# Values put in chunk order by transfers within SBUF instead of by TensorE, in a recurrent attention and token-mixing kernel

## The chip, the cores and the metric

The kernel runs on one core of a Trainium2 chip. The metric is the device time of one execution in microseconds, the median of the runs shown.

## The reference

For 4 batches, 8 heads, 768 tokens and a head size of 48, a recurrence with a decaying state is computed per head; its output, 384 wide per token, goes through a token-mixing layer.

```python
for t in range(S):
    cur = einsum('bhd,bhe->bhde', u[None] * kt, vt)
    y[:, :, t] = einsum('bhd,bhde->bhe', rt, state + cur)
    state = wt[:, :, :, None] * state + einsum('bhd,bhe->bhde', kt, vt)
x = y.transpose(0, 2, 1, 3).reshape(B, S, H * D)
W_tok = scale * einsum('bsd,btd->bst', x @ w_q, x @ w_k)
out = maximum(einsum('bst,btd->bsd', W_tok, x), 0.0) @ w_out
```

Inputs and output are float32. `u` is the bonus, one row of 48 per head.

## The kernel before

**Tiles.** A chunk is 128 tokens, a unit is 256 tokens of all 8 heads of one batch. There are 12 units, three to a batch, numbered n = 0 to 11. For a unit, w, k, r and v are loaded each as a tile of 128 partitions x 768 float32 (`load`, line 301): partition p holds tokens 2p and 2p+1 of every head side by side, so that a row in memory is 384 bytes. In this form a partition holds two tokens and the partitions 0 to 63 hold the first chunk, 64 to 127 the second. The computation wants one chunk of 128 tokens over the 128 partitions, even tokens on partitions 0 to 63 and odd ones on 64 to 127 ("chunk order").

**How w, k and r come there.** ACT takes the logarithm of w (`ln`); a product with a 0/1 matrix (`cw`) sums it along the tokens and puts it in order, and ACT takes both exponentials (`ep`, `en`). POOL casts k and r to bfloat16 (`k16`, `r16`), TensorE transposes them in quarters (`kT`, `rT`), a copy (`ks`) and DVE products (`qT`, `RT`, `KT`; most KT are on POOL) follow.

**How v comes there.** For units 0 to 8 POOL casts the value tile to `v16`, TensorE multiplies it with a permutation (`vp`, lines 585 to 597: four products with `PM`, form "E", or with quarters of the identity, form "e"), and ACT or DVE copies the result from PSUM to `VB` (line 598). For batch 3 (`WHOLE = (3,)`, units 9 to 11) all values of the batch come by `load_whole` (line 306): four transfers of 288 KB with 192-byte rows, one token per row, already in chunk order; POOL casts them to `VB` (line 575). `VB` feeds the state update (`sn`), the output product (`ya`) and, times `dd`, the bonus term `Vd` on POOL (line 618).

**The rest of a unit.** `dps` multiplies qT with the bonus `UB` (line 606), `dd` is its copy; `A` and `AM` are the masked scores, `kb` and `kd` the transposed keys, `sn` and `SB` the state passed to the next chunk, `yi` and `ya` the output in PSUM, `X` (DVE) its scaled sum with Vd, `xt` and `XT` its transpose, `qk` and `QK` the projections. After the third unit of a batch `T`, `TS`, `mx`, `rl`, `fp`, `os` do the mixing layer and `st` stores 384 KB of output for each unit.

**The bonus.** `uT` (line 281) is 128 x 8, filled by two transfers on the ACT queue with one element of 4 bytes a row (line 321); POOL casts it to `UB` (line 436).

**What sets the order.** Every operation is a step of a plan (class `Plan`, line 34). `RANK` gives each step its place in the queue of its engine: E TensorE, A ACT, D DVE, P POOL, S the issues of SP. `ALT` gives, letter by letter, the engine or form of the steps that have a choice; a lower-case e is a form of a TensorE step in quarters, and 30 warming products `z` are either run (E) or left out (e). Each engine works its queue strictly in order, and each waits for what its head step needs. A ring holds the buffers of a kind (`RINGS`, line 267): 4 for each of the loaded tiles, 2 for `v16`, `VB` and most others, 4 for `SB`. SP issues all loads and nearly all stores, in order; a load waits on SP until the ring has a free buffer. The numbers of nanoseconds in the steps serve only to write out the order of the program.

The head of the SP order before: wg0 kg0 rg0 vg0 kg1 wg1 rg1 vg1 wg2 kg2 rg2 vg2; its end: vg8 wg10 rg9 kg9 rg10 wg11 kg10, the four of the whole-batch values, st0, kg11 rg11, stores (w, k, r, v of a unit are wg, kg, rg, vg).

Of the kernel before, what the change touches and what calls it, by code (L numbers as in the profile page):

```python
# [33 lines left out]
class Plan:  # L34
# [51 lines left out]
    def order(self):  # L86
# [85 lines left out]
    3, 0, 0, 0, 5, 18, 0, 0, 21, 1, 2, 0, 0, 0, 1, 0, 0, 2, 0, 0, 3, 0, 0, 1, 3, 4, 4, 4, 2, 5,  # L172
    3, 5, 11, 3, 6, 4, 1, 5, 2, 5, 17, 8, 24, 9, 9, 10, 25, 10, 18, 7, 10, 6, 12, 7, 20, 8, 27,
    11, 30, 37, 33, 31, 15, 73, 31, 82, 32, 6, 0, 0, 4, 0, 0, 7, 0, 0, 8, 0, 0, 9, 6, 7, 26, 11,
    12, 23, 28, 10, 13, 12, 14, 8, 34, 14, 36, 15, 15, 40, 17, 45, 21, 41, 18, 48, 20, 53, 23,
    57, 64, 59, 58, 27, 74, 29, 87, 35, 9, 0, 0, 10, 0, 0, 11, 0, 0, 12, 0, 0, 13, 11, 12, 38,
    16, 17, 39, 42, 16, 18, 19, 14, 13, 47, 20, 49, 22, 18, 55, 24, 60, 25, 56, 22, 61, 26, 68,
    69, 72, 70, 30, 80, 36, 88, 36, 94, 38, 97, 40, 109, 49, 47, 0, 0, 102, 42, 120, 53, 50, 0,
    0, 134, 58, 141, 62, 51, 0, 0, 13, 0, 0, 14, 0, 0, 15, 0, 0, 17, 0, 0, 19, 16, 17, 50, 23,
    21, 63, 66, 25, 28, 29, 20, 19, 71, 28, 77, 33, 23, 75, 32, 79, 34, 76, 30, 81, 35, 85, 37,  # L180
    86, 91, 89, 90, 40, 100, 41, 104, 44, 16, 0, 0, 20, 0, 0, 22, 0, 0, 23, 0, 0, 24, 22, 25,
    67, 26, 27, 84, 93, 38, 42, 41, 39, 26, 95, 39, 110, 47, 32, 98, 47, 106, 49, 92, 37, 101,
    46, 105, 48, 115, 119, 118, 117, 54, 128, 59, 139, 60, 19, 0, 0, 21, 0, 0, 24, 0, 0, 25, 0,
    0, 31, 24, 27, 83, 34, 33, 96, 99, 43, 44, 45, 29, 28, 103, 43, 111, 48, 33, 113, 52, 108,
    50, 107, 45, 112, 51, 122, 124, 126, 125, 57, 138, 61, 156, 68, 164, 73, 167, 76, 185, 82,
    54, 0, 0, 176, 78, 211, 97, 52, 0, 0, 183, 81, 213, 99, 53, 0, 0, 26, 0, 0, 28, 0, 0, 27, 0,
    0, 31, 0, 0, 46, 31, 30, 116, 52, 51, 114, 121, 53, 56, 55, 34, 35, 129, 56, 136, 62, 40,
    131, 60, 140, 65, 127, 58, 135, 61, 143, 68, 149, 151, 153, 154, 73, 165, 75, 188, 86, 29,
    0, 0, 30, 0, 0, 33, 0, 0, 32, 0, 0, 50, 36, 38, 123, 55, 54, 132, 137, 57, 64, 63, 39, 37,
    142, 66, 159, 69, 47, 163, 76, 160, 75, 144, 67, 148, 70, 157, 74, 170, 172, 174, 175, 82,  # L190
    187, 83, 199, 91, 35, 0, 0, 37, 0, 0, 34, 0, 0, 38, 0, 0, 59, 41, 42, 145, 65, 64, 146, 150,
    69, 71, 72, 44, 43, 155, 67, 158, 70, 49, 177, 83, 166, 77, 161, 71, 168, 78, 179, 181, 184,
    182, 86, 191, 89, 205, 94, 212, 98, 223, 103, 237, 109, 55, 0, 0, 231, 105, 245, 111, 56, 0,
    0, 234, 109, 248, 113, 57, 0, 0, 36, 0, 0, 41, 0, 0, 40, 0, 0, 45, 0, 0, 46, 0, 0, 63, 46,
    45, 162, 72, 74, 169, 171, 79, 81, 80, 51, 53, 189, 84, 56, 195, 91, 186, 87, 190, 88, 194,
    90, 198, 92, 200, 203, 201, 204, 95, 210, 96, 221, 102, 39, 0, 0, 44, 0, 0, 42, 0, 0, 66,
    50, 48, 173, 77, 79, 178, 180, 80, 85, 84, 52, 54, 192, 87, 59, 207, 98, 197, 93, 193, 88,
    202, 94, 206, 96, 214, 217, 219, 216, 104, 226, 104, 233, 110, 43, 0, 0, 48, 0, 0, 49, 0, 0,
    85, 55, 57, 196, 92, 89, 93, 90, 208, 209, 95, 102, 99, 97, 100, 101, 58, 220, 101, 60, 61,
    215, 103, 224, 106, 218, 100, 222, 105, 225, 229, 227, 230, 228, 232, 107, 235, 106, 238,  # L200
    239, 112, 111, 108, 236, 107, 240, 241, 108, 113, 242, 244, 243, 110, 246, 114, 115, 250,
    253, 118, 116, 59, 0, 0, 61, 0, 0, 247, 112, 116, 251, 252, 114, 119, 58, 0, 0, 60, 0, 0,
    249, 117, 115, 254, 255, 117, 118, 119, 62, 0, 0, 6, 147, 19, 35, 13, 51, 65, 43, 44, 29,
    16, 2, 46, 78, 0, 21, 152, 52, 1, 62, 130, 32, 15, 8, 14, 54, 22, 9, 133, 7,
]
ALT = ("PPDEADAAEDAPPADEAAEAEAAPPDPEADAeDAAAAAAAAPPAPeADEAEAAPPDDEAAeAEDAPPDPeAAAEAAAAAAAAAPPDPE"
       "ADEDEAAPPAPeDAEDEAAPPDPeAAAEDAAAAAADAPPDPAeDEAAPPAPAEAeADPPAAAEADDEAADADDDAADADDAAAEeEEE"
       "eEEEEEeeEeeeEeeeeEeeEeeeE")
# [5 lines left out]
def kernel(  # L214
# [27 lines left out]
    WHOLE = (3,)  # L242
    DIRECT = (0, N - 1)

# [36 lines left out]
    uT = const([C, NP * 2], F32, "uT")  # L281
    UB = const([C, NP * 2], BF16, "UB")
# [31 lines left out]
    def setup():  # L314
# [4 lines left out]
        nc.vector.memset(uT, 0.0)  # L319
        for hh in range(2):  # L320
            nc.scalar.dma_start(out=view(uT, hh, [[2, NP], [1, 1]], p0=hh * 64, pn=D),
                                in_=dataclasses.replace(u, offset=hh * D,
                                                        ap=[[1, D], [D2, NP], [1, 1]]))
# [30 lines left out]
        nc.vector.memset(PM, 0.0)  # L354
# [62 lines left out]
    def weights():  # L417
        bq = Buf("none")

        def f(e):  # L420
            nc.sync.dma_start(out=view(wq_f, 0, [[DH, NK], [1, DH]]),
                              in_=moe_w_q.rearrange("(n p) h -> p n h", p=128))
            nc.sync.dma_start(out=view(wk_f, 0, [[DH, NK], [1, DH]]),
                              in_=moe_w_k.rearrange("(n p) h -> p n h", p=128))
            nc.sync.dma_start(out=view(wo_f, 0, [[DM, NK], [1, DM]]),
                              in_=moe_w_out.rearrange("(n p) d -> p n d", p=128))
        l = plan.dma(("wts",), 1800, 3300, f)[1]

        def cast(e):
            nc.gpsimd.tensor_scalar_mul(view(wq_sb, 0, [[128, NK], [64, 2], [1, DH]]),  # L430
                                        view(wq_f, 0, [[DH, NK], [0, 2], [1, DH]]), scale)
            nc.gpsimd.tensor_copy(wk_sb, wk_f)
            nc.gpsimd.tensor_copy(wo_sb, wo_f)
        wts["qk"] = wts["o"] = add(("wcast",), {"P": 2650}, cast, [l])
        wts["p"] = add(("pm",), {"P": 900}, lambda e: permute())
        wts["u"] = add(("ub",), {"P": 200}, lambda e: nc.gpsimd.tensor_copy(UB, uT))

    def unit(n, batch):
# [9 lines left out]
        for name, ap in (("wg", w), ("kg", k), ("rg", r)) + (() if whole else (("vg", v),)):  # L448
            g[name] = ring(name)
            g[name + "L"] = plan.dma((name, n), 570, 1190 + 250 * (n == 0 and name == 'kg') + 250 * (n > 2),  # L450
                                     lambda e, ap=ap, x=g[name].tile: load(b, i, x, ap),
                                     buf=g[name])[1]
# [61 lines left out]

        def transposed(name, src, step, place):
            def f(e):
                o = at(kr, BF16)
                for hp in range(NP):
                    for j in range(2):
                        for c in range(2):  # L520
                            mm(o[:, ds(c * 1024 + place + hp * C + j * 64, 64)],
                               src.tile[ds(c * 64, 64), ds(j * 512 + hp * 128, 128)],
                               ID16[ds(c * 64, 64), ds(c * 64, 64)], trans=True)
            return add((name, n), {"E": 245}, f, [step], kr, [src], mode=1)

        def turned(place, c0=0, nc_=2):
            return view(at(kr, BF16), c0 * 1024 + place, [[1024, nc_], [1, 512]])
        kTs = transposed("kT", k16, k16s, 0)
        rTs = transposed("rT", r16, r16s, 512)
# [7 lines left out]
                      view(qT.tile, 0, [[512, 2], [1, 512]]), turned(512),  # L537
# [5 lines left out]
        for cs in fine:  # L543
            n4 = NP * len(cs)

            def f_RT(e, cs=cs, n4=n4):
                o = view(RT.tile, cs[0] * 512, [[512, len(cs)], [64, H], [1, 64]])
                x = view(at(kr, BF16), cs[0] * 1024 + 512, [[1024, len(cs)], [64, H], [1, 64]])
                y = view(ep.tile, cs[0] * NP * EW, [[NP * EW, len(cs)], [66, H], [1, 64]])
                nc.vector.tensor_tensor(o, x, y, ALU.mult)  # L550
# [28 lines left out]
        else:  # L579
            v16, vp = ring("v16"), wide()  # L580
            v16s = add(("v16", n), {"P": 826}, lambda e: nc.gpsimd.tensor_copy(  # L581
                view(v16.tile, 0, [[D, H], [DM, 2], [1, D]]),
                view(g["vg"].tile, 0, [[D2, H], [D, 2], [1, D]])), [g["vgL"]], v16, [g["vg"]])

            def f_vp(e):
                x = at(vp)
                for j in range(2):
                    for c in range(2):
# [7 lines left out]
            vps = add(("vp", n), {"E": (330, 1, None), "e": (185, 3, None)}, f_vp,  # L596
                      [v16s, wts["p"]], vp, [v16])
            VBs = add(("VB", n), copies(2 * DM), lambda e: copy(
                e, view(VB.tile, 0, [[DM, 2], [1, DM]]), view(at(vp), 0, [[512, 2], [1, DM]])),
                [vps], VB, [vp])  # L600
# [3 lines left out]
        def f_dps(e):  # L604
            x = at(dps)
            for c in range(2):
                for hp in range(NP):
                    mm(x[:, ds(c * H + hp * 2, 2)], qT.tile[:, ds((c * NP + hp) * C, C)],
                       UB[:, ds(hp * 2, 2)], start=(c == 0 and hp == 0), stop=True)
# [327 lines left out]
```

## Time and profile before

| | |
|---|---|
| runs, us | 105.81, 105.46, 107.37; median 105.81 |
| profiled execution | 104.84 us, of which the span of the profile is 103.0 |
| busy, us | PE 89.3, DVE 81.9, ACT 80.5, POOL 69.5 |
| granted TensorE clock | 0.973 |
| queue 1 (SP) | 56224 packets, 24.19 MB, 85.0% of 16 engines' span |
| HBM | 19.66 MB read, 4.72 MB written |

Busy times are those of each engine's instructions in the profiled execution; the four engines and the transfers work beside each other, so the times do not add up to the span. A wait costs time only where nothing else fills it.

### The profile page before, as it was taken

To read this page: it belongs to the slowest core of one execution; us is meant where nothing else is said; L and a number is where in the kernel's file an instruction comes from. 1 tells how busy PE (TensorE), PEld (TensorE's weight loads), DVE (VectorE), ACT (ScalarE), POOL (GpSimd) and SP (SyncE) were. 2 spreads that over 40 slices of the span, in tenths; PEclk is the share of its full clock that TensorE was granted. 3 is DMA by queue.
4 is the path that set the end of the run, shared out by engine and by line. 5 is a ranking of instruction groups with operands and counts; after the bars stand their busy time and mean duration, and the time that the engine had idled before them with its cause. 6 is when DMAs were issued, how large, how long until landed. Compare 5 with 4: busy or idle time off the path is not lost.

```text
span 103.0 us, 4462 instructions
## 1 busy us (share of the span) xinstructions
PE 89.3 (87%) x1898; PEld 64.3 (62%) x1898; DVE 81.9 (80%) x140; ACT 80.5 (78%) x121; POOL 69.5 (67%) x81
## 2 busy tenths in 40 slices
PE   5969994999799998999989899879899979999930
PEld 2234753567676966686785787756888648766610
DVE  6628995959989888998999998897999599882800
ACT  6376969769699997999999999888898766766650
POOL 6666393899899976789989997997978504100000
PEclk9999999669999999999999999999999999999995
DMA  1999999999999998999999996999992036204694
GB/s 29 296 325 325 328 259 253 311 296 269 324 255 260 311 293 221 293 282 276 315 314 308 244 293 175 225 166 213 279 376 76 6 153 235 77 0 159 262 353 152
DMA packets 56804, 24.67 MB, mean 240 GB/s; under 512 B 54480, under 2 KB 55632, under 8 KB 56784
## 3 DMA queue, kind: packets, MB, share of 16 engines
q1 hardware_dynamic: 56224, 24.19, 85.0%
q8 instruction: 15, 0.25, 0.9%
q10 hardware_dynamic: 560, 0.20, 0.7%
q14 instruction: 5, 0.04, 0.1%
HBM read 19.66 MB, written 4.72 MB: 237 GB/s over the span
## 4 chain that ended last, share of the span: by engine, by line
PE 51%; DVE 14%; ACT 10%; SPq 9%; DMA 6%; issue 4%; POOL 1%; DVEq 0%; POOLq 0%; ACTq 0%
PE PS L250 51%; SPq L302 9%; DMA kg<-in_k_dram 6%; DVE AM L638 5%; ACT ks L393 3%; DVE X L754 2%; DVE ks L399 2%; ACT ep L500 2%; DVE qT L536 2%; ACT os L393 1%; DVE RT L550 1%; ACT kd L395 1%; ACT en L505 1%; POOL k L472 1%; ACT lw L462 1%
## 5 line engine op out<-in xcount | busy, mean ns | idle before, releaser
L638 DVE TENSOR_TENSOR AM<-PS,US 128x1024 bf16<-128x1024 f32 x24 | 28.9, 1218 | 0.9 <-PE PS L250 0.6
L618 POOL TENSOR_TENSOR Vd<-VB,dd 128x768 bf16<-128x768 bf16 (+1 forms) x14 | 18.0, 1293 | 5.1 <-ACT dd L393 5.1
L560 POOL TENSOR_TENSOR KT<-ks,en 128x1024 bf16<-128x1024 bf16 x8 | 17.0, 2127 | 1.3 <-ACT ks L393 1.3
L500 ACT ACTIVATE ep<-PS 128x1024 bf16<-128x1024 f32 (+1 forms) x14 | 12.6, 918 | 1.7 <-PE PS L250 1.7
L250 PE MATMUL PS<-wo,MX 128*128 128x384 bf16 x72 | 13.4, 326 | 0.7 <-DVE AM L638 0.7
L505 ACT ACTIVATE en<-PS 128x1024 bf16<-128x1024 f32 (+1 forms) x14 | 12.4, 901 | 1.6 <-PE PS L250 1.2
L754 DVE SCALAR_TENSOR_TENSOR X<-PS,gx,Vd 128x768 bf16<-128x768 f32 (+1 forms) x13 | 12.4, 950 | 1.5 <-PE PS L250 1.4
L462 ACT ACTIVATE lw<-wg 128x768 bf16<-128x768 f32 x12 | 10.2, 848 | 4.1 <-DMA wg<-in_w_dram 4.1
L250 PEld LDWEIGHTS <-KT 48*128 48x128 bf16 (+1 forms) x312 | 10.0, 95 | 5.2 <-issue 3.5
L472 POOL CAST k<-kg 128x768 bf16<-128x768 f32 x12 | 9.9, 825 | 4.3 <-DMA kg<-in_k_dram 4.3
L393 ACT COPY os<-PS 128x768 f32<-128x768 f32 (+1 forms) x13 | 9.1, 704 | 3.4 <-PE PS L250 3.2
L472 POOL CAST r<-rg 128x768 bf16<-128x768 f32 x12 | 9.9, 826 | 2.5 <-DMA rg<-in_r_dram 2.4
L250 PE MATMUL PS<-RT,KT 48*128 48x128 bf16 x192 | 9.7, 221 | 0.9 <-DVE qT L536 0.7
L250 PE MATMUL PS<-Z 128*128 128x512 bf16 x23 | 9.2, 502 | 1.2 <-DVE uT L319 1.2
L250 PEld LDWEIGHTS <-MX 128*128 128x128 bf16 x72 | 6.5, 97 | 4.9 <-issue 1.1
L581 POOL CAST v<-vg 128x768 bf16<-128x768 f32 x9 | 7.9, 878 | 2.4 <-DMA vg<-in_v_dram 2.4
L550 DVE TENSOR_TENSOR RT<-PS,ep 128x1024 bf16<-128x1024 bf16 (+1 forms) x14 | 8.3, 607 | 1.0 <-ACT ks L393 0.5
L536 DVE TENSOR_TENSOR qT<-PS,ks 128x1024 bf16<-128x1024 bf16 x12 | 8.2, 682 | 0.9 <-PE PS L250 0.7
L395 ACT ACTIVATE kd<-PS,gk 128x384 bf16<-128x384 bf16 (+1 forms) x10 | 7.0, 712 | 1.7 <-PE PS L250 1.5
L696 DVE TENSOR_TENSOR SB<-PS,ep 128x192 bf16<-128x192 f32 x20 | 7.0, 349 | 1.7 <-PE PS L250 1.5
L250 PE MATMUL PS<-SB,RT 48*128 48x48 bf16 x160 | 7.1, 182 | 1.3
L405 ACT ACTIVATE MX<-PS 128x768 bf16<-128x768 f32 (+1 forms) x10 | 7.5, 753 | 0.7 <-PE PS L250 0.6
(83 smaller groups left out, 188.7 us busy)
## 6 DMA issues: line engine op xcount, KB each, us to landing
wg<-in_w_dram SPq DMA_DIRECT2D x12, 384.0 KB, 5.7
kg<-in_k_dram SPq DMA_DIRECT2D x12, 384.0 KB, 5.9
rg<-in_r_dram SPq DMA_DIRECT2D x12, 384.0 KB, 5.4
vg<-in_v_dram SPq DMA_DIRECT2D x9, 384.0 KB, 5.0
out_dram<-os SPq DMA_DIRECT2D x9, 384.0 KB, 3.1
vw<-in_v_dram SPq DMA_DIRECT2D x4, 288.0 KB, 6.1
out_dram<-os SPq DMA_DIRECT2D x5, 192.0 KB, 2.1
wof<-in_moe_w_out_dram SPq DMA_DIRECT2D x1, 576.0 KB, 5.6
```

The costliest lines, as they stand in the source:

```text
L250: return nc.tensor.matmul(o, l, rr, start=start, stop=stop, skip_group_check=True, is_transpose=trans)
L393: nc.scalar.copy(o, i)
L462: nc.scalar.activation(view(lw.tile, 0, [[64, H], [512, 2], [1, D]]), view(g["wg"].tile, 0, [[D2, H], [D, 2], [1, D]]), ACT.Ln, bias=0.0, ...
L472: op(view(o.tile, 0, [[64, H], [512, 2], [1, D]]), view(g[src].tile, 0, [[D2, H], [D, 2], [1, D]]))
L500: nc.scalar.activation(view(ep.tile, cs[0] * NP * EW + 66, [[EW, NP * len(cs)], [-65, 2], [1, 64]]), at(cw)[:, ds(cs[0] * 512, w_)], ACT.E ...
L505: nc.scalar.activation(en.tile[:, ds(cs[0] * 512, w_)], at(cw)[:, ds(cs[0] * 512, w_)], ACT.Exp, bias=0.0, scale=-1.0)
L536: lambda e: nc.vector.tensor_tensor(view(qT.tile, 0, [[512, 2], [1, 512]]), turned(512), view(ks.tile, 0, [[512, 2], [1, 512]]), ALU.mult),
L550: nc.vector.tensor_tensor(o, x, y, ALU.mult)
L560: x.tensor_tensor(o, view(ks.tile, cs[0] * 512, dims), y, ALU.mult)
L618: nc.gpsimd.tensor_tensor(Vd.tile[:, cols], VB.tile[:, cols], view(dd.tile, cs[0] * H, [[1, len(cs) * H], [0, D]]), ALU.mult)
L638: AMs[c] = add(("AM", n, c), {"D": 1221}, lambda e, c=c, A=A: nc.vector.tensor_tensor(view(AM[c].tile, 0, [[C, 8], [1, C]]), view(at(A), 0 ...
L754: nc.vector.scalar_tensor_tensor(view(X.tile, (2 * i + c0) * DM, [[DM, nc_], [1, DM]]), view(at(y), 0, [[512, nc_], [1, DM]]), gx, view(Vd ...
```

## The change

- Units 3 to 11 (`MOVED`) no longer use `vp` and its copy, and `WHOLE` is empty, so that units 9 to 11 load their values in rows of 384 bytes like all others. For these nine units the value tile is cast to `v16` on POOL, and four transfers from SBUF to SBUF (`f_mv`), each of 64 partitions x 768 bytes, write `VB` directly. They are issued on SP, in its order, and wait there for the cast. Units 0 to 2 keep the permutation on TensorE.
- `FULL`: k and r of units 0 and 1 are transposed with the whole array, 8 products of 128 x 128 for each, instead of in 16 quarters.
- The bonus is loaded as 8 rows (`UR`), cast on POOL (`U16`), transposed on TensorE (`ut`) and copied to `UB`.
- `RANK` and `ALT` are new, so all queues have another order, and steps with a choice may sit on another engine. Among them: the cast of k of unit 0 goes to DVE, four casts of k and r (k of units 2 and 4, r of units 3 and 4) to ACT; ten `ks` copies are on DVE instead of seven; 21 of the 30 warming products `z` run, after 14 (nine more stand at the program's head in both).
- The SP order is now: wg0 kg0 rg0 vg0 wg1 kg1 rg1 vg1 kg2 wg2 rg2 vg2 wg3 wg4 kg3 vg3 rg3, the weights, kg4 mv3 vg4 rg4 wg5 kg5 rg5 vg5 mv4 wg6 kg6 wg7 rg6 vg6 kg7 mv5 rg7 vg7 wg8 kg8 mv6 rg8 kg9 vg8 wg9 mv7 rg9 vg9 rg10 wg10 mv8 kg10 vg10 rg11 st2 kg11 mv9 wg11 st1 st0 vg11 mv10 st3 mv11, stores (mv3 is the four transfers of unit 3).

```diff
-    WHOLE = (3,)
+    WHOLE = ()
+    MOVED = tuple(range(3, N))
+    FULL = (0, 1)
...
-            nc.scalar.dma_start(out=view(uT, hh, [[2, NP], [1, 1]], p0=hh * 64, pn=D),
+            nc.scalar.dma_start(out=UR[ds(hh * NP, NP), ds(hh * 64, D)],
                                 in_=dataclasses.replace(u, offset=hh * D,
-                                                        ap=[[1, D], [D2, NP], [1, 1]]))
+                                                        ap=[[D2, NP], [1, D]]))
...
-        wts["u"] = add(("ub",), {"P": 200}, lambda e: nc.gpsimd.tensor_copy(UB, uT))
+        ut = bank()
+        x = add(("u16",), {"P": 200}, lambda e: nc.gpsimd.tensor_copy(U16, UR))
+        x = add(("ut",), {"E": 60}, lambda e: mm(at(ut)[:, ds(0, H)], U16, ID16[ds(0, H), ds(0, H)]),
+                [x], ut)
+        wts["u"] = add(("ub",), {"A": 200, "D": 160},
+                       lambda e: copy(e, UB, at(ut)[:, ds(0, H)]), [x], reads=[ut])
...
+                        x = src.tile[:, ds(j * 512 + hp * 128, 128)]
+                        if full:
+                            mm(view(o, place + hp * C + j * 64, [[apart, 2], [1, 64]]), x, ID16,
+                               trans=True)
+                            continue
...
-            v16, vp = ring("v16"), wide()
+            v16, vp = ring("v16"), None if n in MOVED else wide()
...
+            def f_mv(e):
+                for j in range(2):
+                    for c in range(2):
+                        nc.sync.dma_start(out=VB.tile[ds(j * 64, 64), ds(c * DM, DM)],
+                                          in_=v16.tile[ds(c * 64, 64), ds(j * DM, DM)])
...
+            if n in MOVED:
+                VBs = plan.dma(("mv", n), 2000, 650, f_mv, [v16s], VB, [v16])[1]
+            else:
```

## The prediction

> **What bounds the kernel now.** I read the page's slices first, then the chain that ended last, then the busy times by stretch.
>
> ```profile
> PE   5969994999799998999989899879899979999930
> DVE  6628995959989888998999998897999599882800
> ACT  6376969769699997999999999888898766766650
> POOL 6666393899899976789989997997978504100000
> DMA  1999999999999998999999996999992036204694
> PE 51%; DVE 14%; ACT 10%; SPq 9%; DMA 6%; issue 4%; POOL 1%; DVEq 0%; POOLq 0%; ACTq 0%
> ```
>
> Each digit is 2.6 us. Up to slice 30 (77 us) the transfers never rest and all four engines stand near 9; after it TensorE alone stays full to 95 us. The chain runs through TensorE for half the span; it leaves the input transfers at 16.6 us, when k of unit 2 lands. By stretch (columns: stretch, length, then busy us and instructions of PE, PEld, DVE, ACT, POOL; granted clock; DMA share; GB/s):
>
> ```profile
> 40.00:50.00 10.00, 9.41 (x238) 7.17 (x236) 9.47 (x13) 9.01 (x14) 9.03 (x8) 1.00 1.04 275
> 50.00:60.00 10.00, 9.23 (x210) 7.07 (x206) 9.38 (x16) 9.45 (x13) 9.66 (x10) 1.00 1.09 290
> 60.00:70.00 10.00, 8.88 (x257) 7.12 (x254) 9.24 (x13) 8.86 (x15) 9.09 (x8) 1.00 0.94 210
> 70.00:76.00 6.00, 5.67 (x131) 4.74 (x132) 5.32 (x9) 5.19 (x9) 4.50 (x5) 1.00 1.04 272
> ```
>
> No engine has more than a tenth to spare between 40 and 70 us. The transfers do: between 6 and 14 us they moved 325 GB/s, here 275 to 290, because SP waits for buffers (the SP queue's own waits at line 302 sum to 15.8 us between 20 and 60 us, 10.0 of it on POOL, the rest on ACT). So inputs and engines pace each other, and then TensorE drains a backlog. The dip to 210 GB/s is the whole-batch value load: in the timeline SP's four issues take 6.72 us.
>
> ```profile
> 62.72 6.72 SPq L309 DMA_DIRECT2D vw<-in_v_dram x4
> wg<-in_w_dram SPq DMA_DIRECT2D x12, 384.0 KB, 5.7
> out_dram<-os SPq DMA_DIRECT2D x5, 192.0 KB, 2.1
> ```
>
> The second and third lines are medians from issue to landing: 5.7 us behind a full queue, 2.1 us behind an empty one.
>
> **The change, part by part.** The profiled execution took 104.84 us: span 103.0 and 1.84 around it. The median shown is 105.81, 0.97 more. I sum on the span and add both.
>
> *TensorE.* The permutation of units 3 to 8 goes (units 9 to 11 had none). Its slots, from each start to the next instruction's start in TensorE's timeline, are 0.28, 0.34, 0.29, 0.46, 0.29 and 0.29 us: 1.95 us. Two of them:
>
> ```profile
> 50.93 0.50 PE L250 MATMUL PS<-v,PM 64*128 64x384 bf16 x4
> 51.39 0.40 PE L250 MATMUL PS<-RT,KT 48*128 48x128 bf16 x8
> 55.97 0.36 PE L250 MATMUL PS<-v,ID 64*64 64x384 bf16 x4
> 56.26 0.26 PE L250 MATMUL PS<-SB,IDU 128*128 128x192 bf16 x1
> ```
>
> All six lie between 29 and 61 us, where TensorE is 92% busy and carries the chain: -1.95, between 0 (all of it turns into waits) and -1.95. Added: the four full-array transposes of units 0 and 1. Eight 128x128 transposes took a slot of 0.45 us at 30.8, sixteen quarter ones 0.23 to 0.34: +0.1 to +0.2 each, up to +0.8; they run while unit 1 and 2 wait for inputs (TensorE's waits for casts and logarithm before 18 us are 0.6 to 1.0 us each), so 0. Warming matmuls rise from 23 to 30 by the order strings; 7 x 0.39 = 2.7 us if their slots were not idle, 0 as placed.
>
> *ACT, DVE, POOL*, counted from the order strings. ACT: VB copies 8 to 3 (5 x 0.796), ks copies 5 to 2 (3 x 1.014), four casts of k and r taken over (no row on ACT; the logarithm on the same tile takes 0.848, so +3.4), all else +1.9: **-1.7**. DVE: ks +3 x 0.686, VB -0.957, one cast of k (between 0.55, its XT copy, and 0.96, its VB cast), all else -1.3: **about +0.3**. POOL: five casts fewer at 0.826: **-4.1**; the values of units 9 to 11 are cast there either way. On the chain, two of its three ACT ks copies (26.47 and 80.48 us) go to DVE, 2 x 0.33 = -0.65; POOL freed in a stretch where SP waits for it, -0.35, an estimate (between 0 and a quarter of the 4.1). Together -1.0, between +0.3 (DVE, no slack, gets the longer list) and -1.7.
>
> *Bonus.* Two row loads on the ACT queue in place of two with 4-byte elements, a small cast on POOL, a transpose, a copy. The bonus is first used at 11.35 us, the old UB was there at 6.02: that slack hides it, 0; with no cover a cast, a product and a copy of 0.2 us each, +0.6.
>
> *Start.* k of unit 0 is cast on DVE instead of on POOL, where it stood behind UB and its 0.77 us wait; k of unit 2 goes one load ahead of w. The chain of that stretch waits for inputs of unit 2, of which the last (v, 19.1 us) keeps its place: 0, between -0.6 and +0.5.
>
> *Transfers.* The whole-batch load moved 1.18 MB at 177 to 195 GB/s (6.0 to 6.7 us); as row loads at 283 to 325 it takes 3.6 to 4.2. A move is 197 KB in 768-byte rows: 0.6 us at 325 GB/s, 1.1 at the 177 of the 192-byte rows; its rows are longer than any load's, so 0.6. Seven moves stand ahead of unit 11's w: 4.2 us (to 7.8). Up to the last of its w, k and r that is about +1.7 us of transfer time (between +1.1 and +6.0), and v of unit 11, two output stores later, is some 3.5 us behind that. In the old trace r of unit 11 was cast by 78.65 and transposed at 80.05, k by 76.44 and at 79.81. So 1.4 to 3.4 us of lateness are covered. Against that, DVE's 1.28 us wait at 81.5 us for ks of unit 11 and PE's 0.67 at 83.1 behind it can shrink, since the whole-batch load no longer stands in front of k and r, and r comes three loads earlier: -0.5, between -0.9 and 0.
>
> *The new wait.* A move is four issues on SP (0.36 us each by the unhindered store row, 1.4 together; 4 x 1.15 = 4.6 if each is held by a full queue as a load is). It waits for the value cast on POOL, and all later loads and stores wait behind it on SP. Value cast to VB took 2.4 to 5.9 us (unit 6: 49.89 to 52.31). Now: cast 0.83, issue 1.4, landing 2.1 to 5.7: 4.3 to 8.0, so VB comes some 3 us later, and sn, ya and Vd with it. VB stood ready only 0.4 to 3.6 us ahead of sn (unit 6: 0.4). The new TensorE order puts other steps in front; POOL's puts the value cast of units 5 to 10 ahead of the Vd of the unit before, so that no move waits for the one before it; units 4 and 11 have Vd ahead. Cost +1.0, one wait of a third of the 3 us in each of the three later batches; between 0 and +5 (nine waits of about 0.6).
>
> The Trainium skill, "DMA: Bandwidth & Descriptors", section "Rules for kernel authors", says that transfers under 64 KB pay mostly overhead and should be merged; a move's four are 48 KB each. The row nearest to it: the two 96 KB weight loads flew with others between 24 and 30 us and the transfers still moved 314 GB/s in 26 to 30. By the page's 0.95 us for 64 KB a move would hold the wires 3.8 us, an estimate, and the seven 27 us.
>
> Sum: -1.95 - 1.0 - 0.5 + 1.0 = -2.45. Span 100.55, own time 102.4, against the median **103.4 us**, 2.3% under it.
>
> **Rivals.**
> *A, no gain (0.24).* VB of unit 10 comes late. Its move stands behind v of unit 11, the last load, in SP's order. At the old pace the last of k, w and r lands at 77 us, and two stores, v and the move follow (3.5 + 0.6): VB is there at 81 us. In the old order sn of unit 10 ran at 77.8; the new one puts 2.4 us of other work ahead of it (yi, ya, qk, a score product, the transposes of unit 11, T: slots of 0.2 to 0.7 each) and the gains take 2.45 away again, so TensorE would wait some 3 us there in place of the 1.0 of the sum: 105.8 - 3.45 + 3 = 105.3, and 104.5 to 107 around it. For it: TensorE is the chain from 72 us on. Against: the freed POOL lets the loads run ahead of the old pace, and each microsecond there comes off this wait; I allow two of the three.
> *B, slower (0.25): SP blocks the inputs.* Today 15.8 us of SP waits go with a fall from 325 to about 285 GB/s over 40 us, some 5 us of transfers lost: a third of each held us. Seven moves that hold SP 1.4 us of issue and 1.5 us for the cast (one or two POOL instructions of 0.83 to 2.13 stand in front) hold it 20 us, 6.4 us lost; with the 1.7 of added transfers unit 11 comes 8 us late, 3 us of that covered by slack, 2.5 by the gains: +2.8, 108.6. It decides when the last of w, k and r of unit 11 lands after 81 us. For it: the transfers never rest up to 77 us. Against: a queue 5.7 us deep rides out short holds, and POOL has 4 us less.
> *C (0.04): each of the 36 small transfers takes the wires alone* for 1.5 us (the 2.1 of a store in an empty queue less its 0.6 of data): 7 moves x 4 x 1.5 = 42 us, of which the lost 5 and the 3 of slack hide little: over 125. This is where the page's rule on small transfers would lead; 314 GB/s beside the weight loads speaks against it.
> *D (0.09): the inputs run free.* Freed POOL casts remove the SP waits; half of the 5 us lost comes back: 103.4 - 2.5 = 100.9.
>
> **How the numbers follow.** Forecast 0.38, its own range 101.8 to 104.6. A measurement of this kernel tells about 2% from no change, so faster is under 103.7 and slower over 107.9. Faster: D, 0.27 of the forecast's, 0.06 of A and 0.03 of B, should their waits be short: 0.45. Slower: 0.22 of B, C and 0.05 of A: 0.31. The rest, 0.24, is within. The range runs from 100.6 (D with the low ends) to 109.3 (B and some of its upper part), leaving out C, the tail of B and a little below.
>
> **What would show it.** Right: no TensorE work on PM after 20 us; POOL near 65, ACT near 79, DVE near 82 us; move landings 2 to 6 us after issue; the input rate between 62 and 72 us over 260 GB/s; TensorE busy without waits over 0.5 us on VB. B shows as SP waits of line 302's neighbours on the value cast summing to over 8 us and last inputs after 81 us; A as TensorE waits on moved VB in units 9 to 11. The forecast is wrong if the span is above 102 us.

## The result, and the profile after

The changed kernel took **114.38 us** (median of four runs, 113.27 to 115.99) against 106.03 for the kernel before. The ratio is 1.077, with a 95% interval from 1.065 to 1.089: slower by 8%, where 103.4 was forecast. (Ratios here compare undisturbed runs only; medians are over all runs of a kernel.) The profiled execution took 113.27 us with a span of 111.4, 8.4 more than before.

From the page of the changed kernel, in the order in which the page of before was read: busy slices (2.8 us each), transfers, and the chain that ended last.

```profile
PE   5988898999978797883995989729979999999950
POOL 5645755999989569436865993895569452300000
DMA  2999999999799949974989939949989540028395
GB/s 54 321 323 325 327 278 263 297 253 303 191 298 301 259 108 325 324 205 123 324 228 233 314 104 295 314 104 323 357 270 292 158 136 24 6 92 332 151 373 185
PE 35%; DMA 20%; SPq 13%; POOL 8%; issue 8%; ACT 7%; DVE 6%; POOLq 0%; ACTq 0%; DVEq 0%
```

The row to look at is DMA. Before, it never rested up to 77 us; now it has holes in the steady part, and the rate in them falls to values like 108, 123 and 104 GB/s, with up to 325 on either side. The holes come about once per unit. TensorE's share of the chain fell from 51% to 35%, and transfers and SP's queue rose from 15% to 33%. By stretch (columns as in the prediction):

```profile
40.00:50.00 10.00, 8.53 (x196) 6.10 (x194) 8.76 (x13) 8.15 (x13) 6.62 (x6) 1.00 0.93 254
50.00:60.00 10.00, 6.69 (x128) 5.00 (x128) 5.97 (x8) 6.27 (x10) 7.06 (x7) 0.83 0.85 229
60.00:70.00 10.00, 9.52 (x256) 7.82 (x254) 9.05 (x13) 7.66 (x13) 7.13 (x7) 1.00 0.89 238
70.00:76.00 6.00, 3.29 (x85) 2.66 (x79) 2.82 (x5) 2.83 (x5) 4.75 (x4) 0.78 0.80 218
```

All four engines went slack together: between 50 and 60 us none is busy for more than 7.1 of 10. When everything idles at once, look for what feeds everything. Next, who waits (columns: total us, times, longest), from the chain of waits of all engines and of SP's queue:

```profile
POOL r L485 <- DMA rg<-in_r_dram: 9.3, 8, 2.1
ACT lw L475 <- DMA wg<-in_w_dram: 5.9, 7, 1.7
POOL k L485 <- DMA kg<-in_k_dram: 5.2, 6, 1.3
POOL v L604 <- DMA vg<-in_v_dram: 5.2, 6, 1.7
PE PS L254 <- DMA VB<-v: 5.2, 4, 2.6
```

```profile
SPq L611 <- POOL r L485: 6.1, 5, 2.3
SPq L611 <- POOL v L604: 2.2, 2, 1.5
```

Waits for inputs on POOL and ACT sum to 25.6 us; before, the four sums (4.3, 4.1, 2.4, 2.4) made 13.2. TensorE waits for moved values 5.2 us. The second list has to be read beside SP's timeline. Its rows at line 611 sum to 10.7 us, but only the 2.2 us on the value cast, ahead of the moves of units 3 and 11, are gaps in which SP issued nothing. The other 8.5 us lie inside long issues: POOL or TensorE happened to finish something while an issue was running, and the view counts that as a wait. The values of unit 5, for one, had been cast by 40.86 us, and their move was issued at 45.42.

What a move does to SP and to the wires is best seen at one of them, that of unit 5. SP's timeline, then the move's line (ns: least, median, longest of the 36 issues), then the same time in half microseconds:

```profile
43.01 1.15 SPq L307 DMA_DIRECT2D vg<-in_v_dram  x1
44.20 1.11 SPq L307 DMA_DIRECT2D kg<-in_k_dram  x1
45.42 4.53 SPq L611 DMA_DIRECT2D VB<-v  x4
50.05 0.88 SPq L307 DMA_DIRECT2D rg<-in_r_dram  x1
50.97 0.58 SPq L307 DMA_DIRECT2D vg<-in_v_dram  x1
```

```profile
L611 SPq DMA_DIRECT2D VB<-v x36: 461/594/2608, 26.5 to 90.8; - x36
```

```profile
48.00:48.50 0.50, 0.24 (x16) 0.24 (x15) 0.50 (x2) 0.50 (x2) 0.00 (x0) 1.00 1.15 320
48.50:49.00 0.50, 0.50 (x20) 0.45 (x12) 0.26 (x2) 0.40 (x1) 0.00 (x0) 1.00 0.69 181
49.00:49.50 0.50, 0.50 (x21) 0.48 (x19) 0.50 (x2) 0.35 (x1) 0.12 (x1) 1.00 0.30 79
...
51.00:51.50 0.50, 0.00 (x0) 0.00 (x0) 0.00 (x0) 0.00 (x0) 0.32 (x1) 1.00 0.03 3
51.50:52.00 0.50, 0.22 (x9) 0.22 (x10) 0.00 (x0) 0.00 (x0) 0.00 (x0) 1.00 0.48 93
52.00:52.50 0.50, 0.50 (x17) 0.47 (x13) 0.24 (x1) 0.00 (x0) 0.40 (x1) 1.00 0.73 172
52.50:53.00 0.50, 0.50 (x22) 0.48 (x21) 0.50 (x2) 0.34 (x1) 0.50 (x1) 0.83 1.17 327
```

A load of 384 KB holds SP for 1.15 us, about what its bytes take at 325 GB/s; behind the move, with the wires nearly empty, the same issue took 0.58. The first transfer of the move, 48 KB, held SP for 2.61 us, and the three behind it 0.59 each, though the bytes of one take 0.15 us. When the first issue ended, at 48.03, the wires had about half a microsecond of work left. From 49.0 to 51.0 they carried 79 to 102 GB/s, and after that 3. The load issued at 50.05 first shows at 51.5 and fills the wires from 52.5 on. The hole is some 4 us, and at 51.0 every engine but POOL stands still.

The Trainium skill, "DMA: Bandwidth & Descriptors", section "Issuing engines are not separate DMA queues", calls the time that a sequencer takes to start a transfer "usually small relative to the DMA itself". The trace agrees where the whole transfer is meant, 0.59 us against 3.7 from issue to landing. Against the time of the bytes it differs: for 48 KB the issue took four times as long.

The lateness adds up to the end: k of unit 11 was cast at 84.50 us, against 75.61 before.

### The profile page after: what moved, and what is told of

The parts are those of the page before. It is cut to its first block, busy times and chain, and to the rows that moved or that the text cites. A ratio compares the mean times of both kernels' runs of the same rounds, so it can differ in the third digit from the quotient of the medians.

```text
span 111.4 us, 4391 instructions
## 1 busy us (share of the span) xinstructions
PE 92.9 (83%) x1842; PEld 67.3 (60%) x1842; DVE 84.4 (76%) x138; ACT 78.9 (71%) x123; POOL 66.2 (59%) x76
## 4 chain that ended last, share of the span: by engine, by line
PE 35%; DMA 20%; SPq 13%; POOL 8%; issue 8%; ACT 7%; DVE 6%; POOLq 0%; ACTq 0%; DVEq 0%
PE PS L254 35%; DMA wg<-in_w_dram 9%; SPq L307 8%; DMA VB<-v 6%; POOL KT L583 6%; DMA kg<-in_k_dram 5%; SPq L611 4%; ACT os L399 3%; DVE AM L670 2%; DVE X L786 2%; ACT lw L475 1%; ACT XT L399 1%; POOL v L604 1%; DVE ks L405 1%; POOL k L485 1%
## 5 line engine op out<-in xcount | busy, mean ns | idle before, releaser
L650 POOL TENSOR_TENSOR Vd<-VB,dd 128x768 bf16<-128x768 bf16 (+1 forms) x14 | 18.5, 1324 | 4.7 <-ACT dd L399 3.1
L254 PEld LDWEIGHTS <-KT 48*128 48x128 bf16 (+1 forms) x304 | 10.8, 97 | 5.3 <-issue 2.1
L485 POOL CAST r<-rg 128x768 bf16<-128x768 f32 x10 | 8.3, 826 | 9.6 <-DMA rg<-in_r_dram 9.3
L254 PE MATMUL PS<-wo,MX 128*128 128x384 bf16 x72 | 13.2, 326 | 0.2 <-DVE X L786 0.2
L604 POOL CAST v<-vg 128x768 bf16<-128x768 f32 x12 | 9.9, 828 | 5.3 <-DMA vg<-in_v_dram 5.2
L254 PE MATMUL PS<-VB,kd 128*128 128x48 bf16 x160 | 7.4, 185 | 6.7 <-DMA VB<-v 5.2
L254 PE MATMUL PS<-Z 128*128 128x512 bf16 x30 | 11.0, 456 | 1.4 <-DVE Z L321 1.2
L254 PEld LDWEIGHTS <-kd 128*128 128x128 bf16 x160 | 6.4, 97 | 8.8 <-DMA VB<-v 5.2
L485 POOL CAST k<-kg 128x768 bf16<-128x768 f32 x9 | 7.4, 827 | 5.2 <-DMA kg<-in_k_dram 5.2
L399 ACT COPY os<-PS 128x768 f32<-128x768 f32 (+1 forms) x12 | 8.2, 691 | 2.0 <-PE PS L254 1.4
L254 PE MATMUL PS<-VB,AM 128*128 128x48 bf16 x192 | 8.8, 190 | 0.0
```

Source lines behind the costliest of these rows:

```text
L254: return nc.tensor.matmul(o, l, rr, start=start, stop=stop, skip_group_check=True, is_transpose=trans)
L399: nc.scalar.copy(o, i)
L485: op(view(o.tile, 0, [[64, H], [512, 2], [1, D]]), view(g[src].tile, 0, [[D2, H], [D, 2], [1, D]]))
L650: nc.gpsimd.tensor_tensor(Vd.tile[:, cols], VB.tile[:, cols], view(dd.tile, cs[0] * H, [[1, len(cs) * H], [0, D]]), ALU.mult)
```

## The experiments

The table sums up the thirteen kernels; the edits and what was expected of each follow. "Transfers" counts the small ones added for units 3 to 11. Seven kernels (a_nomove, b_scratch, c_tiny, v_early, e_nowait, u_half, t_spreadscratch) leave the values of these units out of chunk order, so they do not compute the layer and serve only to separate causes.

| kernel | transfers | median us | ratio to before, 95% |
|---|---|---|---|
| changed kernel | 36, four in a row, SP | 114.38 | 1.077 [1.065, 1.089] |
| a_nomove | none | 103.09 | 0.977 [0.967, 0.986] |
| b_scratch | 36 to a scratch tile | 114.02 | 1.067 [1.051, 1.083] |
| c_tiny | 36, an eighth of the bytes | 115.26 | 1.080 [1.061, 1.099] |
| v_early | 36, of the unit before | 113.46 | 1.067, no interval |
| e_nowait | 36, of a constant tile | 117.67 | 1.110 [1.098, 1.121] |
| u_half | 18 to scratch, two in a row | 105.36 | 0.998 [0.992, 1.004] |
| t_spreadscratch | 36 to scratch, one at a time | 109.92 | 1.040 [1.028, 1.051] |
| s_spread | 36 real, one at a time | 115.97 | 1.098 [1.086, 1.109] |
| d_diag | 18 real, two in a row | 111.38 | 1.052 [1.039, 1.065] |
| f_poolq | 36 real, on POOL's queue | 118.77 | 1.125 [1.119, 1.131] |
| h_rows | none; 36 row loads of 96 KB | 114.00 | 1.069 [1.056, 1.081] |
| w_whole | none; 12 row loads of 288 KB | 116.92 | 1.108 [1.097, 1.119] |
| i_turn | none; permutation on TensorE | 109.60 | 1.039 [1.031, 1.047] |

**Is it the moves?** In a_nomove the cast writes `VB` and nothing is moved; b_scratch puts the 36 transfers back, into a tile that nobody reads.

```diff
 a_nomove:
-    VBs = plan.dma(("mv", n), 2000, 650, f_mv, [v16s], VB, [v16])[1]
+    VBs = v16s          # the cast writes VB, four VB buffers
 b_scratch, on top of it:
+    plan.dma(("mv", n), 2000, 650, f_mv, [v16s], None, [VB])   # VB -> scratch
```

> The changed kernel without its 36 moves: POOL casts v of units 3 to 11 straight into VB (four VB buffers), so the order of tokens within VB is left out for these units; every other step stands in the changed order. Theory H1 (SP is held by the moves and the inputs behind them come late), H2 (VB lands late at sn, ya and Vd) and H3 (the moves' data slow the loads on the wires) all put the loss into the moves: 103 to 105 us. Theory H4 (the new step order is itself the loss): 109 or more.

> As a_nomove, but the 36 moves are issued on SP at their places in the changed order, from VB into scratch tiles that nobody reads. Nobody waits for a move; SP and the wires have the whole of it. H1: 111 to 114 us, and SP is held 2.4 us or more by each group of four. H2: 103 to 105 us. H3: between 106 and 112.

Measured 103.09 and 114.02 us. The DMA row of a_nomove's page, and the cast of k of unit 11 from POOL's timeline:

```profile
DMA  1999999999899999999999997999996000065793
```

```profile
74.60 0.83 POOL L485 CAST k<-kg 128x768 bf16<-128x768 f32 x1
```

Without moves the wires are full to 77 us, and the last k is cast 9.9 us earlier than the changed kernel's 84.50. The spans differ by 10.0 (101.4 and 111.4). So the moves cost the whole loss. Without them the new order came out 2.3% under before (interval 1.4 to 3.3%), but it does less than the result needs and has four `VB` buffers in place of two. b_scratch, with the same four buffers, gives most of the loss back although nobody waits for what it moves (ratio 1.067 of the changed kernel's 1.077), and it casts k of unit 11 at 83.34 us: the inputs are late there too. By the ratios about a tenth of the loss can be lateness of `VB`, and the intervals allow up to a third. In the changed kernel that lateness does stand on the chain (`VB` transfers are 6% of it), but taking it away gains little: in b_scratch input transfers are 29% of the chain, against 14% in the changed kernel.

**The bytes, or the wait for the cast?** c_tiny moves 48 of the 384 columns. v_early moves `VB` of the unit before, which is long there. e_nowait moves a constant tile.

```diff
 c_tiny:
-    out=SC[...][ds(j * 64, 64), ds(c * DM, DM)]
+    out=SC[...][ds(j * 64, 64), ds(c * DM, D)]
 v_early:
-    plan.dma(("mv", n), 2000, 650, f_mv, [v16s], None, [VB])
+    plan.dma(("mv", n), 2000, 650, f_mv, [VBold[0]], None, [VBold[1]])
```

> As b_scratch, but each move carries 48 of 384 columns, an eighth of the bytes in as many rows and issues. H1: as b_scratch within 1 us. H3: as a_nomove within 1.5 us.

> As b_scratch, but the four transfers at the place of unit n carry VB of unit n-1, which has long been cast, so that SP does not wait for a cast at a move; nothing is added at the start. H1a: 112 to 115 us, as b_scratch. H1b (the wait for the cast is the loss): 103 to 106 us.

> As b_scratch, but the 36 moves carry zeros from a tile set at the start to scratch, so that SP waits for no cast and for no buffer before a move: issues and data alone. Theory H1a (four issues of 0.6 us each, in which no load is issued, empty the queue): 110 to 113 us. Theory H1b (the wait for the value cast on POOL holds SP): 103 to 106 us, and the low slices of the input rate are gone.

Measured 115.26, 113.46 and 117.67. An eighth of the bytes saves nothing (c_tiny came out 1.2 us above b_scratch, just outside its range). The issue line of c_tiny beside that of the full moves above tells why:

```profile
L613 SPq DMA_DIRECT2D SC<-VB x36: 461/595/2617, 26.7 to 90.7; - x36
```

Nearly the same three numbers, for 6 KB as for 48: SP pays by the transfer, not by the byte. Taking the wait for the cast away (v_early) changes nothing that these runs can tell. e_nowait says the same less cleanly: it fills its constant tile at the start, and its first small transfer is issued at 28.98 us, against 26.3 in b_scratch. Its 117.67 lies above both of its ranges. Its longest issue is 2.62 us, although no transfer waits for a cast there: the long issue at a move is not a wait for the cast.

**The number, or the row of four?** u_half leaves out two of the four transfers. t_spreadscratch issues all four, each behind another load; s_spread does that with the real moves.

```diff
 u_half:
-    for c in range(2):
+    for c in range(1):
 t_spreadscratch, s_spread (up to unit 9):
-    one step of four transfers
+    four steps of one transfer, placed a step of SP's order apart
```

> As b_scratch, with two transfers for a unit in a row instead of four, 18 in all, half of the bytes. H1a: two in a row leave 1.2 us of issue for 0.3 us of data; well under half of the loss of four: 104.5 to 108.5 us. H1c (only the first of a group costs): as b_scratch, 111 to 114.

> As b_scratch (36 transfers of v to scratch that nobody reads), but on SP the four of a unit stand singly, each with a load behind it, up to unit 9. Theory H1a (a transfer takes SP and its queue 0.6 us whatever its size, and four in a row leave the wires with 0.6 us of data for 2.4 us or more; one alone is covered by the 1.2 us of data of the loads around it): 103.5 to 107 us. Rival H1c (a transfer out of SBUF is not taken until the loads ahead of it have left, each time): 116 us or more.

> The changed kernel, whole computation, with its four moves of a unit singly on SP, each with a load behind it, up to unit 9 (four VB and three v16 buffers). H1a: the inputs come in time, VB some three loads (3.6 us) later than with moves in a row; if that is covered 104 to 108 us, if it is not 108 to 111. H1c: 116 us or more.

Measured 105.36, 109.92 and 115.97. With none, two and four in a row per unit the ratio to before is 0.977, 0.998 and 1.067: the first pair costs 2.2 us over all units, the second 7.3. SP's timeline of u_half has holds of 1.1 to 2.5 us per pair, that of the changed kernel 2.4 to 4.5 per four, mostly over 3; loads took 4.5 to 4.8 us from issue to landing there. The short holds are ridden out on what is already queued, the long ones mostly leave a hole. No run varied the length of a hold alone. The DMA rows of the pages of u_half and of t_spreadscratch:

```profile
DMA  1999999999999999998989989899999100056694
```

```profile
DMA  2999999999997998999799999999998651037495
```

Spread singly, the 36 leave no deep hole, and by the ratios 2.9 of the 9.6 us come back; 109.92 lies outside both of its ranges. The rest, 6.7 us, stays. SP's rows in the timeline between 20 and 76 us fill 53.0 of 56 us without moves (a row of several issues takes in the gaps between them), all of it loads and stores; in t_spreadscratch they fill 50.5, of which 23.6 is the small transfers. A filled row is not time that SP needs: most loads without moves hold it for over 1 us, and behind a small transfer most take 0.53 to 0.66. So the loads give back part of what the small transfers take. How 23.6 us of them become 6.7 us at the end was not settled. s_spread loses 6 us more than its twin: there TensorE waits 8.9 us for `VB`, whose last quarter comes some loads later. Its 115.97 lies between its ranges.

**Fewer issues, or another queue.** d_diag moves only the two quarters that change partitions, and POOL casts the other two into `VB`. f_poolq issues the four on POOL's queue, right behind the cast.

```diff
 d_diag:
-    one cast of 128 x 768, four transfers
+    four casts of 64 x 384, two transfers
 f_poolq:
-    nc.sync.dma_start(out=VB.tile[...], in_=v16.tile[...])
+    nc.gpsimd.dma_start(out=VB.tile[...], in_=v16.tile[...])
```

> The whole computation with half of the moves: the quarters whose tokens stand on the right partitions already are cast by POOL straight into VB (three VB buffers), only the two others are cast to v16 and moved, 18 issues in all; POOL's value cast becomes four casts of 64 partitions, some 0.9 us more per unit. H1: half of the loss comes back, 108 to 110 us. H2: VB lands at most 1.2 us earlier and POOL is longer, so 112 to 115 us. H4: 113 to 116 us.

> The changed kernel with its moves on POOL's queue, each group right behind its value cast (three VB buffers), the whole computation. Theory H1 (SP's order is what costs): 104 to 107 us, if four issues take POOL no more than 1 us together. Rival (POOL's issues cost as much as SP's, and POOL has casts and products behind them): 110 or more, and POOL full from 30 to 80 us.

Measured 111.38 and 118.77. d_diag lies between the ranges of H1 and H2, f_poolq where its rival put it. d_diag's input rate is mostly 250 to 320 GB/s again, but its four casts take 2.2 us of POOL in place of 0.83. POOL is busy for 44.7 of the 48 us between 40 and 88 there, and TensorE waits for its `KT`. In f_poolq the price of an issue went along to the other engine (POOL's timeline, then the chain of waits):

```profile
43.93 2.09 POOL L611 DMA_DIRECT2D VB<-v  x4 [0.30 <-POOL v L604]
```

```profile
PE PS L254 <- POOL KT L583: 9.4, 5, 3.0
```

Four issues take 2.09 us of POOL, 36 of them 18.8; its busy time is 85.0 in place of 66.2. The wires have no holes (240 to 358 GB/s between 18 and 73 us), and POOL sets the pace.

**Values straight from memory.** h_rows loads the values of units 3 to 11 in rows of 192 bytes, in chunk order, by four transfers of 96 KB per unit. w_whole loads the same rows a batch at a time.

```diff
 h_rows:
+    def load_rows: four transfers per unit, 64 rows of partitions x 8 heads x 192 bytes
 w_whole:
+    load_whole for batches 1 to 3, each half next to the value load that it replaces
```

> The whole computation without moves: values of units 3 to 11 are loaded in rows of 192 bytes, four transfers for a unit, straight in chunk order, and cast by POOL into VB (four buffers). Theory H1: SP has as many issues as with moves but none that waits for an engine, and each carries a quarter of a load; the rows cost some 0.7 us more on the wires for a unit, 6.7 us for nine, part of it in the idle time of the transfers: 104 to 107 us. Rival (any extra issue on SP costs its time): 109 to 112 us.

> The whole computation in the changed order, with no moves. The values of units 3 to 11 come straight in chunk order in rows of 192 bytes, as in the kernel that loaded them unit by unit (114.0 us), byte for byte and row for row the same, but a batch at a time: 12 transfers of 288 KB in place of 36 of 96 KB. POOL casts them into VB. Theory (the number of small transfers that SP has to issue holds the inputs): with a third of the issues and no four small ones in a row, the holes in the input rate (111, 89, 128 and 114 GB/s there) fill up, and the time falls to 104.5 to 108, the price of the short rows included (3.5 MB at 177 to 195 GB/s in place of 283 to 325, 5 to 8 us of transfers, part of it covered). Rival 1 (the short rows were what cost the 114.0): the same bytes in the same rows give the same time, 112 to 115. Rival 2 (a long issue is as bad: the before kernel's four took 6.72 us of SP): holes of the same depth, three of them and longer, 110 to 112.

Measured 114.00 and 116.92. Both lie above all of their ranges. My theory said 104.5 to 108 for w_whole and fell: a third of the issues did not bring the time back, so rival 1, the short rows, is nearest. It is not shown, since loading a batch at a time also puts values that are needed late ahead of loads that are needed soon. Slices of w_whole's page:

```profile
DMA  2999999999999999999599989989993000018394
GB/s 46 323 316 325 321 283 213 240 280 186 254 306 288 285 185 280 247 194 230 141 245 258 190 203 205 189 209 312 299 364 120 0 6 0 0 74 344 141 374 180
```

The wires hardly rest, and carry 185 to 258 GB/s for much of the time. The last k is cast at 86.34 us. This is another loss than that of the moves: there the wires were empty, here they are full and slow. It also means that h_rows, with the same rows and holes down to 89 GB/s besides, does not tell the two apart, and is no evidence for the price of an issue.

**The old way in the new order.** i_turn puts the permutation of `vp` back on TensorE with its copy on ACT or DVE.

```diff
-    if n in MOVED: move
+    vp = four products ahead of kb; copy to VB ahead of kd
```

> The changed order with the old way for the values: units 3 to 11 are permuted on TensorE (in quarters) ahead of kb, and copied to VB by ACT or DVE ahead of kd; no moves, three VB buffers, the whole computation. It has 9 slots of 0.29 us on TensorE (2.6 us) and nine copies more than a_nomove: 104 to 107 us if all else of the change is worth nothing against the kernel before, 101 to 103 if the permutation was hidden.

Measured 109.60, above both ranges. Where the two steps stand was my choice, and at one place POOL waited 6.8 us for `VB` behind it. This does not say what the best order with the permutation would give. No kernel with the whole computation was faster than the one before.

## Why the prediction was wrong

**What bounds the kernel.** The prediction had inputs and engines pace each other, from 15.8 us in which SP was said to wait for buffers between 20 and 60 us. That was the same misreading as at the moves. SP's timeline has no gap over 0.2 us in that stretch, and its rows fill 53.6 of the 56 us between 20 and 76. The longest wait that the view counts there, 2.5 us "on POOL r", lies inside this issue of k of unit 10:

```profile
59.63 3.04 SPq L302 DMA_DIRECT2D kg<-in_k_dram  x1
44.16 0.83 POOL L472 CAST k<-kg 128x768 bf16<-128x768 f32 x1 [0.97 <-DMA kg<-in_k_dram]
```

The second line is the cast of k of unit 6, which freed the buffer 14.6 us before the issue. No load of the kernel before found its buffer freed less than 8 us ahead. So the engines did not hold the inputs back. The loads set the pace, and whatever delays their issue delays everything behind them. Why some loads hold SP for 2 to 3 us is open.

**The gains: about right as a sum.** It had -1.95 for TensorE, -1.0 for the other engines and -0.5 for the tail, 3.45 in all. a_nomove holds all three without the wait, and came out 2.5 us under before by its ratio (1.5 to 3.5). No run separates the three, a_nomove has two more `VB` buffers, and the 0.35 us for POOL "in a stretch where SP waits for it" had no such wait behind it, so some of the agreement may be luck. The engines' busy times are as forecast: POOL 66.2 (65), ACT 78.9 (79), DVE 84.4 (82); moves landed in 3.7 us (2 to 6).

**The step that failed: the new wait, +1.0 (0 to +5).** It was the only term of the sum in which a move's issues stood, and it was costed as lateness of `VB`. Its issue was taken from the unhindered store row, 0.36 us each and 1.4 together. Measured: 0.46 to 0.60 for most, up to 2.61 for the first, 24.0 us for the seven moves ahead of unit 11's w in place of 9.8. Its true size was about 11 us (114.38 less 103.09; 10.7 by the two ratios), and b_scratch shows that little of it is lateness of `VB`: SP's issues at the moves emptied the wires, and the inputs came late. The end at 4.6 us for four issues stood in the text ("if each is held by a full queue") and was not carried into the input side. That the bytes of a move are cheap was right (c_tiny).

**"Transfers" at nothing.** The 1.4 to 3.4 us of lateness that unit 11 had to spare were to cover 1.7 us. The holes brought k of unit 11 8.9 us later than before, so the cover was spent several times over.

**Rival B had the place right, half of the cause and too small a price.** SP blocks the inputs, and the last of them did come after 81 us (84.5). Its price was 108.6. It had seven moves hold SP 9.8 us by their issues and 10.5 by waits for the cast. The issues took 24.0, and the waits ahead of them 1.5, all at unit 3. Its sign, over 8 us of waits on the value cast, did not show: 2.2 us are real. Its factor, a third of each held microsecond lost, came from the 15.8 us that were no waits; with the measured 25.5 us it gives about 110. What spoke against it, "a queue 5.7 us deep rides out short holds", holds for two transfers in a row (u_half), not for four: at the end of the first issue of the move of unit 5 the wires had about half a microsecond left, not five.

**Rival C**, by the rule of the Trainium skill on small transfers ("DMA: Bandwidth & Descriptors", "Rules for kernel authors"), pointed at the right item with another price. The estimate from the page's figure was 3.8 us per move on the wires. The hole at unit 5 is near that, but it comes from SP's issues: c_tiny, with an eighth of the bytes, shows that it is the number that pays, and f_poolq's full wires show that the transfers themselves can run beside others.

**Rivals A and D.** A's sign hardly showed: of the 5.2 us in which TensorE waited for moved values, 0.6 are in units 9 to 11. For D there was no wait of SP to remove; without moves k of unit 11 is cast only 1.0 us earlier than before.

**Not in the sum at all:** TensorE's clock. Behind the idle stretches the granted clock reads 0.83 and 0.78, and TensorE was busy 92.9 us for 1842 instructions that took 89.1 in a_nomove (clock 0.952 and 0.994). Some of the loss at the end may be this; no run separates it.

## What to carry to other kernels

Where the wires never rest, compare for each transfer how long its issue holds the issuing engine with how long its bytes occupy the wires. A load here held SP 1.15 us for 1.2 us of bytes, a row of four small ones 2.4 to 4.5 us for 0.6 us. The loads already queued cover a short deficit (two in a row), not a long one (four). Check a wait that a view reports against the timeline of the engine that is said to wait: if its rows leave no gap, look when what it is said to wait for was really done. A move that takes work off a compute engine is no free copy, and changing its queue only changes who pays.

## What the runs showed of the hardware that was not expected

- An issue on SP took 0.46 to 0.6 us for 48 KB and for 6 KB alike (median 0.594 and 0.595), and one of a row behind full loads, mostly the first, up to 2.6 us. On POOL it took 0.52 us (0.516 to 0.713).
- When that long issue ended at unit 5, the wires had about 0.5 us of work left; after the hole, a load took 1.5 us from the start of its issue to its first bytes and 2.5 to the full rate. Why the first one is held so long no run settled.
- With the values of nine units in rows of 192 bytes the wires hardly rested between 45 and 75 us and moved mostly 189 to 258 GB/s; with all loads in rows of 384 bytes mostly 244 to 305 (w_whole and a_nomove).
